# A one-column exponential ahead of ScalarE's DMA issues, and one weight slice issued by SyncE instead of ScalarE

## The chip, the core and the metric

The kernel runs on one core of one Trainium2 chip. The metric is the device time of one execution in microseconds (us), from several executions of the same program; the median is compared. The core has five engines that work in parallel, each with an instruction stream of its own: TensorE (PE, matrix products and transposes), VectorE (DVE), ScalarE (ACT, element functions such as exp and gelu, each from a function table that must be loaded), GpSimd (POOL) and SyncE (SP, which here only issues transfers). Engines meet through semaphores. A transfer (DMA) between the chip's memory and the core's on-chip memory is issued by an instruction of SyncE, ScalarE or GpSimd and carried out by sixteen DMA engines that all queues share.

## The reference: what is computed

The input x has 2048 rows (tokens) of 640 values. Two branches are computed from it and mixed by a gate per token, g = sigmoid(sum(x * gate_w)):

```
q, k, v   = x @ wqkv, in 32 heads of 20;  phi(t) = (t+1 if t>0 else exp(t)) + 1e-6
branch A  = ((phi(q) @ (phi(k)^T v)) / (phi(q) . sum phi(k) + 1e-6)) @ wo
h         = gelu(layernorm(x) @ w1), its four column groups shifted by 1, -1, 2, -2 tokens
x1        = x + h @ w2
branch B  = x1 + gelu(layernorm(x1) @ w3) @ w4
out       = g * A + (1 - g) * B
```

All tensors are bf16; sums run in float32.

## The kernel before, in words

Tokens are worked in 16 tiles of 128 rows, and in four chunks of four tiles where a weight stands still in TensorE. Weights of 640 input rows are cut in five slices of 128 rows. First come the products for q and k (with exp on ScalarE and the rest of phi on VectorE), then the sums over tokens of branch A, then w1 and w2 of branch B, then w3, and last the products with w4 and with the folded matrix of branch A, which add into the same result.

How the order is made: the class `_Sched` records every operation with its reads and writes, derives the semaphore waits from them, and keeps a rough cost for each (a cost model, in `simulate`). The class `_Items` lists work items in streams with dependences and takes, step by step, the item that can start soonest by these costs. The stream "A" (q and k) is a fixed order. An exp whose table is not the one last used is costed 1290 ns more in `activation` (the variable `act_func`). Each engine gets its instructions in the order in which they were recorded; a semaphore wait in a stream holds what stands behind it in that stream.

The beginning, which the change touches, is written out by hand, ahead of the planner:

- `load_x(t)` issues the 160 KB of tile t of x on SyncE; `load_wq(k, queue)` issues 128 KB (the first 512 columns of slice k of the q weights, tile `wq`) on the queue named; `load_wk(k, queue)` 160 KB of the k weights (tile `wkg`). `x_turn(t)` has a DMA transpose x tile t into `xT`, on SyncE, and waits for that tile.
- SyncE's order is x0, x1, wq2, x2, wk0, wk2, x3, wk4, x4, then turn 3 (which waits for x3), x5, turn 4, and chunks of x with their turns. ScalarE's is wq0, wq1, wq3, wq4, wk1, wk3, and the last 128 columns of all wq slices in one transfer (here called wqt); then its own computing begins. GpSimd issues the small row gate_w.
- Beside it TensorE runs dummy products (`warmup`, line 904) and then `t_x` (line 637), which transposes an x tile by a product with the identity; VectorE copies the result into `xT` (line 691). Tiles 0 to 2 go this way, later ones by `x_turn`.
- `q_three` (line 942 through `stream`) is a hand-written order of q's products for tiles 0 to 2, one step per tile and slice:

```
order = [(0, 0), (1, None), (0, 1), (1, 0), (1, 1), (0, 2), (1, 2), (0, 3), (1, 3), (2, None), (0, 4), (1, 4),
         (2, 0), (2, 1), (2, 2), (2, 3), (2, 4)]
```

Here (t, k) is tile t times slice k, which needs wq slice k and the transposed part k of tile t, and (t, None) is the transposes of tile t, which need x tile t. TensorE works this list in order: a step that waits holds all behind it. Then `k_two` does tiles 0 and 1 of k in the same manner, and single tiles follow.
- `phi` does exp on ScalarE out of PSUM (line 682) and two VectorE operations.

Lines 281 and 285 are the helper that issues DMAs (transposes and plain ones); all of them carry these line numbers.

Of the kernel before, what the change touches and what calls it, by code (L numbers as in the profile page):

```python
# [6 lines left out]
F32 = mybir.dt.float32  # L7
ACTF = mybir.ActivationFunctionType
# [408 lines left out]
def _build(nc, A_x, A_wqkv, A_wo, B_w1, B_w2, B_w3, B_w4, gate_w, out, dbg=None, stop=None):  # L417
# [66 lines left out]
    junk = pa.alloc("junk", [128, 1, D], BF16)  # L484
# [78 lines left out]
    def nfree(ap):  # L563
        n = 1
        for d_ in ap.shape[1:]:
            n *= d_
        return n

    def in_psum(ap):
        return ap.tensor.name == ps.name  # L570

    def act(fn, reads, writes, cost=None):
        if cost is None:
            n = nfree(writes[0])
            cost = max(150.0, 100.0 + 0.833 * n + (70.0 if (reads and in_psum(reads[0])) else 0.0))
            cost += 45.0 * max(0, len(reads) - 1)
        return sch.op("act", fn, reads, writes, cost=cost)

    def dve(fn, reads, writes, cost=None):
        if cost is None:  # L580
            n = nfree(writes[0])
            cost = 65.0 + n / 0.96
        return sch.op("dve", fn, reads, writes, cost=cost)
# [85 lines left out]
    def activation(out_ap, in_ap, func, scale=1.0, bias=0.0, accum=None):  # L669
        rd = [in_ap] + [a for a in (scale, bias) if not isinstance(a, (int, float))]  # L670
        wr = [out_ap] + ([accum] if accum is not None else [])
        n = nfree(out_ap)
        cost = max(150.0, 100.0 + 0.833 * n + (70.0 if in_psum(in_ap) else 0.0)) + 45.0 * (len(rd) - 1)
        if accum is not None:
            cost += 91.0
        st_ = ACT_SET.get(func)
        if st_ is not None and st_ != sch.act_func:
            cost += 1290.0
            sch.act_func = st_
        if accum is not None:  # L680
            return act(lambda e: e.activation(out_ap, in_ap, func, bias=bias, scale=scale, accum_out=accum), rd, wr, cost=cost)  # L681
        return act(lambda e: e.activation(out_ap, in_ap, func, bias=bias, scale=scale), rd, wr, cost=cost)  # L682
# [16 lines left out]
    def dma_in(out_ap, in_ap, key, **kw):  # L699
        return sch.dma("sp", out_ap, in_ap, key, **kw)  # L700

    def load_x(t):
        dma_in(x_tok[:, t, :], x2[128 * t:128 * (t + 1), :], "x%d" % t)

    def load_wq(k, queue):
        sch.dma(queue, wq[:, k, 0:512], A_wqkv[128 * k:128 * (k + 1), 0:512], "wq%d" % k)
# [6 lines left out]

    gwr = xn[:, 1, 0:128]
    dve(lambda e: e.memset(gwr, 0.0), [], [gwr])
    load_x(0)
    load_wq(0, "act")
    load_x(1)
    load_wq(1, "act")
    load_wq(2, "sp")  # L720
# [730 lines left out]
def bass_gated_mix__linear_attn_block__mixer_s_mlp__prompt_kernel(  # L1451
    nc, A_x, A_wqkv, A_wo, B_x, B_w1, B_w2, B_w3, B_w4, gate_w, out
):
    assert tuple(A_x.shape) == (1, S, D) and tuple(out.shape) == (1, S, D)
    assert tuple(A_wqkv.shape) == (D, 3 * D) and tuple(A_wo.shape) == (D, D)
    assert tuple(B_w1.shape) == (D, D) and tuple(B_w2.shape) == (D, D)
    assert tuple(B_w3.shape) == (D, F) and tuple(B_w4.shape) == (F, D) and tuple(gate_w.shape) == (D,)
    _build(nc, A_x, A_wqkv, A_wo, B_w1, B_w2, B_w3, B_w4, gate_w, out)
# [28 lines left out]
```

## Time and profile before

| | us |
|---|---|
| median of three runs | 258.79 (258.46 to 259.11) |
| the profiled execution | 259.12 |
| its span, first to last instruction | 257.9 |
| TensorE busy | 254.6 (99% of the span) |
| VectorE / ScalarE / GpSimd busy | 144.1 / 108.5 / 90.6 |
| first product of q's list starts | 4.32 |
| x tile 2's transposes start | 7.28 |
| function table loads on ScalarE | 2 of 1.28, at 4.14 and at 68.30 |

The span of the profile lies 1.2 us under the execution's own time. A profile names engines as PE, PEld (weight loads of TensorE), DVE, ACT, POOL and SP; SPq and ACTq are the queues of SyncE and ScalarE, where a line is the issue of a DMA and not its transfer. In a timeline a line has the start, the length, the engine, the line of the kernel, the operation, out<-in with the shapes, how many were merged, and in brackets how long the engine had been idle before it and what released it. Matmuls are pipelined, so the length of one is longer than the distance to the next.

### The profile page before, as it was taken

To read this page: it belongs to the slowest core of one execution; us is meant where nothing else is said; L and a number is where in the kernel's file an instruction comes from. 1 tells how busy PE (TensorE), PEld (TensorE's weight loads), DVE (VectorE), ACT (ScalarE), POOL (GpSimd) and SP (SyncE) were. 2 spreads that over 40 slices of the span, in tenths; PEclk is the share of its full clock that TensorE was granted. 3 is DMA by queue.
4 is the path that set the end of the run, shared out by engine and by line. 5 is a ranking of instruction groups with operands and counts; after the bars stand their busy time and mean duration, and the time that the engine had idled before them with its cause. 6 is when DMAs were issued, how large, how long until landed. Compare 5 with 4: busy or idle time off the path is not lost.

```text
span 257.9 us, 3612 instructions
## 1 busy us (share of the span) xinstructions
PE 254.6 (99%) x1418; PEld 110.6 (43%) x1242; DVE 144.1 (56%) x290; ACT 108.5 (42%) x222; POOL 90.6 (35%) x146
## 2 busy tenths in 40 slices
PE   8999999999999999999999999999999999999997
PEld 4333333344454333334444444444444444444444
DVE  2697888899953995489999400689300043200033
ACT  1486676751356867665854230003520100253000
POOL 5021399967762153758907100423000011300000
DMA  6767698545843699362915520022300112200002
GB/s 209 223 170 197 145 144 223 172 86 127 108 99 78 97 335 382 85 106 51 124 40 127 127 54 20 0 82 73 51 0 0 23 20 102 102 1 3 0 20 102
DMA packets 57825, 26.48 MB, mean 103 GB/s; under 512 B 49188, under 2 KB 56397, under 8 KB 57808
## 3 DMA queue, kind: packets, MB, share of 16 engines
q1 hardware_dynamic: 54976, 21.87, 35.9%
q0 software_dynamic: 1168, 3.28, 4.9%
q10 hardware_dynamic: 1664, 1.11, 1.4%
q8 instruction: 10, 0.16, 0.3%
q14 instruction: 7, 0.06, 0.1%
HBM read 12.04 MB, written 2.62 MB: 57 GB/s over the span
## 4 chain that ended last, share of the span: by engine, by line
PE 96%; DMA 2%; SPq 0%; DVE 0%; issue 0%
PE ps L606 37%; PE ps L1240 30%; PE ps L625 14%; PE ps L831 7%; PE ps L614 4%; DMA x_tok<-in_A_x_dram 2%; PE ps L942 1%; PE ps L1286 1%; PE ps L1147 1%; SPq L285 0%; PE ps L1029 0%; PE ps L1058 0%; PE ps L637 0%; DVE x_tok L665 0%
## 5 line engine op out<-in xcount | busy, mean ns | idle before, releaser
L606 PE MATMUL ps<-xnT,w 128*128 128x512 bf16 x360 | 81.3, 379 | 0.0
L665 DVE SCALAR_TENSOR_TENSOR x_tok<-ps,stg,abx 128x512 bf16<-128x512 f32 (+2 forms) x17 | 12.2, 719 | 81.5 <-PE ps L1240 81.3
L682 ACT ACTIVATE h2T<-ps 128x512 bf16<-128x512 f32 x52 | 30.6, 598 | 59.3 <-PE ps L606 59.3
L606 PEld LDWEIGHTS ps<-xnT,w 128*128 128x128 bf16 x360 | 34.5, 98 | 41.6 <-issue 2.2
L1240 PE MATMUL ps<-w,h2T 128*128 128x512 bf16 (+2 forms) x221 | 45.4, 366 | 0.0
L648 POOL TENSOR_SCALAR xn<-x_tok,st 128x640 bf16<-128x640 bf16 x32 | 35.3, 1110 | 27.8 <-DMA xnT<-xn 27.2
L648 POOL TENSOR_SCALAR abx<-x_tok,stg 128x640 f32<-128x640 bf16 (+1 forms) x16 | 14.8, 930 | 70.0 <-DVE x_tok L665 70.0
L1240 PEld LDWEIGHTS ps<-w,h2T 128*128 128x128 bf16 x221 | 21.1, 98 | 24.1
L682 ACT ACTIVATE Er<-ps 128x512 bf16<-128x512 f32 (+1 forms) x36 | 23.0, 648 | 14.8 <-PE ps L614 10.6
L681 ACT ACTIVATE junk<-x_tok 128x640 bf16<-128x640 bf16 x32 | 23.6, 738 | 3.9 <-DVE x_tok L663 3.7
L682 ACT ACTIVATE hsT<-ps 128x512 bf16<-128x512 f32 (+1 forms) x32 | 19.0, 593 | 12.6 <-PE ps L606 12.1
L625 PE MATMUL ps<-w,hsT 128*128 128x512 bf16 x80 | 23.0, 379 | 0.0
L625 PE MATMUL ps<-wkg,xT 128*128 128x512 bf16 x70 | 20.6, 379 | 0.0
L663 DVE SCALAR_TENSOR_TENSOR x_tok<-ps,x_tok 128x640 bf16<-128x640 f32 x16 | 13.2, 822 | 10.8 <-PE ps L614 10.2
L1240 PE MATMUL ps<-M_sb,pqnT 128*128 128x512 bf16 (+2 forms) x85 | 18.6, 367 | 0.0
L831 PE MATMUL ps<-pk_tok,x_tok 128*128 128x512 bf16 x80 | 17.8, 379 | 0.0
L614 PE MATMUL ps<-wkg,xT 128*128 128x130 bf16 x80 | 17.6, 220 | 0.0
L1176 DVE TENSOR_TENSOR pq_tok<-pq_tok,dnr 128x300 bf16<-128x300 bf16 (+1 forms) x48 | 17.3, 415 | 0.6
L614 PE MATMUL ps<-w,hsT 128*128 128x128 bf16 x80 | 17.5, 219 | 0.0
L606 PE MATMUL ps<-wq,xT 128*128 128x512 bf16 x65 | 16.2, 379 | 0.0
L648 DVE TENSOR_SCALAR Er<-Er 128x512 bf16<-128x512 bf16 (+1 forms) x36 | 12.2, 340 | 6.8 <-ACT Er L682 5.9
L656 DVE TENSOR_TENSOR qprod<-qprod,pk_tok 128x640 f32<-128x640 f32 x13 | 15.1, 1165 | 0.4
(90 smaller groups left out, 252.4 us busy)
## 6 DMA issues: line engine op xcount, KB each, us to landing
w<-in_B_w_dram SPq DMA_DIRECT2D x1, 2160.0 KB, 8.1
w<-in_B_w_dram SPq DMA_DIRECT2D x1, 2080.0 KB, 13.1
out_dram<-x_tok SPq DMA_DIRECT2D x3, 640.0 KB, 3.1
w<-in_B_w_dram POOLq DMA_DIRECT2D x8, 160.0 KB, 3.4
x_tok<-in_A_x_dram SPq DMA_DIRECT2D x6, 160.0 KB, 4.1
x_tok<-in_A_x_dram SPq DMA_DIRECT2D x1, 960.0 KB, 5.5
wv<-in_A_wqkv_dram POOLq DMA_DIRECT2D x1, 800.0 KB, 5.3
x_tok<-in_A_x_dram SPq DMA_DIRECT2D x1, 640.0 KB, 5.0
```

Source lines behind the costliest of these rows:

```text
L606: ins = e.matmul(out_ap, l, r, start=(i == 0), stop=(i == n - 1))
L614: return e.add_instruction(mybir.InstMatmult(name=nc.get_next_instruction_name(), engine=e.engine, ins=[e.lower_ap(r), ll], outs=[e.lower_ ...
L625: e.matmul(outs[0], l, r, start=st, stop=sp, skip_group_check=True)
L648: return engf(lambda e: e.tensor_scalar(out_ap, in_ap, s1, s2, op0, op1), rd, [out_ap], cost=cost)
L656: return engf(lambda e: e.tensor_tensor(out_ap, a, b_, op), [a, b_], [out_ap], cost=cost)
L663: return dve(lambda e: e.scalar_tensor_tensor(out_ap, in0, scalar, in1, op0, op1, accum_out=accum), rd, [out_ap, accum], cost=cost + 70.0)
L665: return dve(lambda e: e.scalar_tensor_tensor(out_ap, in0, scalar, in1, op0, op1), rd, [out_ap], cost=cost)
L681: return act(lambda e: e.activation(out_ap, in_ap, func, bias=bias, scale=scale, accum_out=accum), rd, wr, cost=cost)
L682: return act(lambda e: e.activation(out_ap, in_ap, func, bias=bias, scale=scale), rd, wr, cost=cost)
L831: ins = e.matmul(o, l, r, start=(t0 + q_ == 0), stop=(t0 + q_ == NT - 1))
L1176: dve(lambda e, o=o, i0=i0, i1=i1: e.tensor_tensor(o, i0, i1, ALU.mult), [i0, dnr[:, 1, sd, :]], [o], cost=cost)
L1240: ins = e.matmul(o, l, r, start=first and i == 0, stop=last and i == len(prs) - 1, skip_group_check=True)
```

## The change

A one-column exponential of a constant zero is put ahead of ScalarE's DMA issues, into the scratch tile `junk`, whose contents nobody reads. So the first instruction of ScalarE that needs a table stands ahead of its first DMA issue. And wq's slice 0 is issued by SyncE behind x tile 0, where ScalarE issued it first of all.

```
     gwr = xn[:, 1, 0:128]
     dve(lambda e: e.memset(gwr, 0.0), [], [gwr])
+    activation(junk[:, 0, 0:1], nc.const_aps.tensor(0.0, [128, 1], F32), ACTF.Exp)
     load_x(0)
-    load_wq(0, "act")
+    load_wq(0, "sp")
     load_x(1)
     load_wq(1, "act")
     load_wq(2, "sp")
```

With it SyncE's order begins x0, wq0, x1, wq2, x2, wk0, and ScalarE's is table load, exponential, wq1, wq3, wq4, wk1, wk3, wqt.

More of the change, by code (lines that the diff above doesn't have):

```diff
@@ L715, in _build @@
     dve(lambda e: e.memset(gwr, 0.0), [], [gwr])
+    activation(junk[:, 0, 0:1], nc.const_aps.tensor(0.0, [128, 1], F32), ACTF.Exp)
     load_x(0)
-    load_wq(0, "act")
+    load_wq(0, "sp")
     load_x(1)
```

## The prediction

> **What bounds the kernel now.** I read the page's busy times first, then who TensorE waited for over the whole span, then the chain of work that ended last, and then the first 14 us instruction by instruction.
>
> ```profile
> PE 254.6 (99%) x1418; PEld 110.6 (43%) x1242; DVE 144.1 (56%) x290; ACT 108.5 (42%) x222; POOL 90.6 (35%) x146
> ...
> PE ps L904 <- PEq L1472: 0.8, 1, 0.8
> PE ps L637 <- DMA x_tok<-in_A_x_dram: 0.6, 1, 0.6
> ```
>
> The first line is the page's; the other two are the complete list of TensorE's waits. TensorE is the bound, and it has two waits: 0.8 us for the program's start, and one for a transfer of x. By the distances between its matmuls it loses nothing more than a tenth of a microsecond at a time from 7.3 us to its end. So whatever delays TensorE in the first 9 us comes out at the end in full, and no change of the opening can gain more than the second wait and a few tenths around it.
>
> ```profile
> 2.18 5.05 DMA x_tok<-in_A_x_dram
> 7.28 0.45 PE ps L637 x5
> 7.74 1.82 PE ps L942 x8
> ```
>
> The chain shows the wait: x tile 2, issued at 2.18, lands 5.05 us later, and its transposes (L637) start at 7.28. The last product before them started at 6.35 (trace) and products stand 0.216 apart, so the gap is 7.28 - 6.56 = 0.72 us.
>
> ```profile
> 0.79 0.87 SPq L285 DMA_DIRECT2D x_tok<-in_A_x_dram  x2
> 0.79 1.86 ACTq L285 DMA_DIRECT2D wq<-in_A_wqkv_dram  x4
> 1.71 0.43 SPq L285 DMA_DIRECT2D wq<-in_A_wqkv_dram  x1
> 2.18 0.43 SPq L285 DMA_DIRECT2D x_tok<-in_A_x_dram  x1
> 2.66 0.91 SPq L285 DMA_DIRECT2D wkg<-in_A_wqkv_dram  x2
> 4.14 1.28 ACT L682 ACT_TABLE_LOAD   x1 [4.14 <-issue]
> 8.01 1.09 ACT L682 ACTIVATE Er<-ps 128x512 bf16<-128x512 f32 x2 [2.59 <-PE ps L942]
> ```
>
> The timeline shows two queues issuing side by side, one DMA per 0.47 us each, and the table load as soon as ScalarE's seven issues are over. It ends at 5.42; the first exp waits for TensorE until 8.01.
>
> ```profile
> x_tok<-in_A_x_dram SPq DMA_DIRECT2D x1, 160.0 KB, 3.1
> wq<-in_A_wqkv_dram SPq DMA_DIRECT2D x1, 128.0 KB, 3.6
> ...
> x_tok<-in_A_x_dram SPq DMA_DIRECT2D x1, 160.0 KB, 5.1
> wkg<-in_A_wqkv_dram SPq DMA_DIRECT2D x1, 160.0 KB, 5.5
> wq<-in_A_wqkv_dram ACTq DMA_DIRECT2D x1, 128.0 KB, 5.3
> ```
>
> These are DMA issues with the time to landing (issues in flight around 1.6 us, then around 2.5 us): x1 and wq2, then x2, wk0 and wq4. Issue plus latency gives landings, and the n-th DMA of SyncE lands together with the n-th of ScalarE: x0 3.7 with wq0 3.8; x1 4.4 with wq1 4.6; wq2 5.3 with wq3 5.6; x2 7.3 with wq4 7.5; wk0 8.16 with wk1 8.3. I call these slots 1 to 5. From 2 us on the DMA engines are 93 to 112% busy by windows of 1 us, so a landing is set by the bytes that go before it on both queues, not by its issue.
>
> **The change part by part.**
>
> *The table load and the exponential.* The load (1.28 us) leaves 4.14 and comes to about 0.79. This gains nothing: ScalarE waits 2.59 us for TensorE ahead of its first exp even now. The exponential itself is bounded by 0.17 us (the two-column copy of lr, 174 ns). What hides both is ScalarE's idleness until 8.01; uncovered they would cost 1.45 us. The question is what they do to the six DMA issues that now stand behind them.
>
> *ScalarE's six issues (wq1, wq3, wq4, wk1, wk3, wqt).* No row before has an issue behind a table load. One end: the issues don't wait, and wq1 is issued at about 0.9 instead of 1.23. The other: they wait until the engine is ready again. The second table load bounds that from above, as the next ACTIVATE began 71.14 - 68.30 = 2.84 us after it started:
>
> ```profile
> 68.30 1.28 ACT L682 ACT_TABLE_LOAD   x1
> 71.14 0.60 ACT L682 ACTIVATE hsT<-ps 128x512 bf16<-128x512 f32 x1 [1.56 <-PE ps L606]
> ```
>
> In the middle lies a hold of the load and the exponential, 1.28 + 0.17 = 1.45 us, with wq1 issued at about 2.2. I take no hold. The nearest records are the trace's semaphore instructions of ScalarE: one is done at 29.19, while the read of an accumulator that stands ahead of it in the stream starts only at 29.39, and one at 11.57, with an ACTIVATE running from 11.56 to 12.26. So ScalarE's instruction stream runs on ahead of its computing, and a DMA issue is, like them, an instruction that needs no function unit.
>
> The Trainium skill agrees with this row and speaks against the change: Trace Analysis, "DVE / Act Engine Instruction", has the sequencer push such an instruction into a queue and fetch the next, and its section on DMA instructions starts an issue on the sequencer once its semaphores are there. By this rule the hold is 0. Another page (ScalarE: Activation LUTs, "What ACT_TABLE_LOAD costs") speaks of 2.66 us with a drain; were the issues behind that, wq1 would go out at 3.5 us. No run here shows either for a DMA issue.
>
> *wq0 moves to SyncE.* One more issue on SyncE moves x1, wq2, x2, wk0, wk2, x3, wk4 and x4 by 0.47 us each, which alone is little. But each moves back by a slot too. SyncE's order becomes x0, wq0, x1, wq2, x2: x2 goes from slot 4 to slot 5, where wk0 is now. The five slots hold the same bytes as before (288 + 256 + 288 + 288 + 320 = 1440 KB against 288 + 288 + 256 + 288 + 320), so slot 5 ends at the same 8.16. Along `q_three`, which TensorE works in order:
> - (0,0) needs wq0, slot 2: 4.4 to 4.5 instead of 3.8, used at 4.32. About 0.1 late.
> - (1,None) needs x1, slot 3: 5.3 instead of 4.4, used at 4.39. 0.9 late, and wq1, which came earlier, waits with all behind it.
> - (0,2) needs wq2, slot 4: 7.3 instead of 5.3, used at about 5.7. Then four steps at 0.216, so (1,3) ends at 7.3 + 0.86 = 8.16.
> - (2,None) needs x2, slot 5: 8.16. Both are there at once, and the transposes start at 8.16 instead of 7.28: **0.88 us** late.
>
> Behind it nothing is added: wq4 has landed a slot earlier, wk0 lands in slot 6 (8.9, where wk2 is) for a use at 9.2 + 0.88, and wk4 at 10.6 (where x4 is) for 11.1 + 0.88. On SyncE turn 3 waits for x3, which goes from 9.5 to slot 8, 10.1 (where wk4 is). Turn 3 thus moves from 9.55 by 0.6, and so do x5, turn 4 and the chunks behind it; turn 3 lands at 12.6 instead of 12.0, and TensorE wants it at 13.2 + 0.88. SyncE's extra issue is hidden by its idleness from 5.2 to 9.5. GpSimd's issue of gate_w is passed by nothing.
>
> *Sum:* 0 (table, exponential) + 0.88. On the profiled execution 259.12 + 0.88 = 260.0; that one was 0.33 above the median, so by the median 258.79 + 0.88 = **259.67**. Ends of this case: 0.6, if the slowest DMA engine is less behind (half of x2's sixteen parts had landed by 6.1, the last at 7.23), and 1.1, if wq2 lands with the later partner of its slot (7.5).
>
> **The rivals.**
>
> *The issues are held for 1.45 us (not slower).* With wq1 at 2.2 SyncE has the DMA engines alone until data of ScalarE's start to flow, about 1.2 us after an issue (wq0, issued at 0.79, has its first packets near 2.0). SyncE's delay of one DMA (128 KB at half of some 330 GB/s, 0.8 us) is made good by a hold of 0.8 us, and that is the point from which this rival decides. Then x2 lands near 6.8; wq1 lands 3.3 us after its issue (its latency now) at 5.5 instead of 4.6; seven steps to (1,3) end at 5.5 + 1.51 = 7.0, x2's transposes start 0.25 early, and (0,4) waits for wq4, issued at 3.2 and due at 7.4 to 7.8 (now 7.60). Between -0.25 and +0.2: 258.5 to 259.0. For it speaks that ScalarE's first load started just after the issues ended, in stream order; against it the semaphore records.
>
> *They are held for up to 2.84 us.* wq1 at 3.7, landing at 6.7 to 7.0; seven steps to 8.2 to 8.5, transposes and (0,4) at 8.5 to 8.8 instead of 7.60: +0.9 to +1.2, 259.7 to 260.0. Nothing in the rows needs so long a hold.
>
> *TensorE's pace stays slow.* Five transposes take 0.71 us at 3.71 and 0.44 us at 4.64: the pace doubles near 4.5 us, after 3.7 us of unbroken work, though the granted clock reads 1.00 throughout. In my forecast TensorE idles from about 4.6 to 5.3, right there, and again ahead of wq2. If the faster pace doesn't come or is lost, four steps after wq2 take 0.43 each, +0.86, and the rest of q's list, nine products, up to 9 x 0.21 = 1.9 more: 260.5 to 262.4.
>
> The Trainium skill (TensorE: Matmul & The Clock Gate, Part 1) has the gate judge activity over free-running windows of about 3.4 us, and close after an idle one. No window here would be wholly idle, so by that rule the pace once gained is kept.
>
> *The planner writes another order.* Its costs now put the 1290 ns of the table ahead and ScalarE's issues later, so a later item can change its place. As TensorE has no waits to give up behind 9 us, this could only lose; 0 to 1 us, 258.8 to 259.8.
>
> **How the numbers follow.** No hold 0.55; short hold 0.28; long hold 0.07; slow pace 0.06; another order 0.04. A measurement can tell about 0.3% here, 0.78 us. No hold (0.6 to 1.1, mid 0.88) is over it two times in three: 0.36 slower, 0.19 same. Short hold: 0.24 same, 0.02 each side. Long hold 0.045 slower, 0.025 same. Slow pace: slower. Another order 0.025 slower, 0.01 same, 0.005 faster. Sums: slower 0.51, same 0.46, faster 0.03. The likeliest case's own range is 259.4 to 259.9; the range must take in the short hold down to 258.4, and above it the long hold and some of the slow pace, to 260.5.
>
> **What would show it.** In the changed profile: a first line of ScalarE's queue near 0.9 (no hold), 2.2 or 3.7; the table load near 0.79 and the first exp still released by TensorE; x2 landing near 8.1 and L637's third group of transposes starting there, with TensorE's waits in sum about 0.9 us longer, on x1, wq2 and x2; transposes of tile 1 at 0.056 or 0.107 apart. I am wrong if ScalarE's first issue comes after the table load: then x2's transposes start at or before 7.3 and the time stays.

## The result and the profile after

| | before | after |
|---|---|---|
| median of 12 runs each, us | 259.07 (258.32 to 259.48) | 259.89 (259.49 to 261.56) |
| ratio, 95% interval | | 1.0049 (1.0031 to 1.0067) |
| the profiled execution / its span | 259.12 / 257.9 | 261.08 / 259.8 |

The changed kernel is slower: +0.82 us between the medians, and by the ratio 259.07 x 0.0049 = 1.27 us (0.8 to 1.7). The two numbers differ because the runs after lie in two groups: seven from 259.49 to 259.91, one at 260.45, and four from 260.94 to 261.56. The runs before have one group. The profiled execution after, 261.08, belongs to the upper one.

The beginning of its timeline, ScalarE and its queue, and SyncE's queue:

```profile
0.79 1.28 ACT L682 ACT_TABLE_LOAD   x1 [0.79 <-PEq L1473]
0.79 0.40 SPq L285 DMA_DIRECT2D x_tok<-in_A_x_dram  x1
0.86 1.35 ACTq L285 DMA_DIRECT2D wq<-in_A_wqkv_dram  x3
1.26 0.41 SPq L285 DMA_DIRECT2D wq<-in_A_wqkv_dram  x1
1.71 0.43 SPq L285 DMA_DIRECT2D x_tok<-in_A_x_dram  x1
2.08 0.21 ACT L682 ACTIVATE junk<-const-float32-0.0 128x1 bf16<-128x1 f32 x1
2.18 0.43 SPq L285 DMA_DIRECT2D wq<-in_A_wqkv_dram  x1
2.23 0.94 ACTq L285 DMA_DIRECT2D wkg<-in_A_wqkv_dram  x2
2.66 0.43 SPq L285 DMA_DIRECT2D x_tok<-in_A_x_dram  x1
...
10.10 1.08 ACT L682 ACTIVATE Er<-ps 128x512 bf16<-128x512 f32 x2 [7.82 <-PE ps L943]
```

ScalarE's queue starts at 0.86, 0.07 us behind the start of the table load and 1.2 us ahead of its end: the load doesn't hold the DMA issues behind it. The exponential follows at 2.08, as soon as the load ends. ScalarE then idles 7.82 us until TensorE has something for it. (The Trainium skill, ScalarE: Activation LUTs, "What ACT_TABLE_LOAD costs", counts a drain of 1.38 us to such a load; here 0.01 us lie between the load and the next ACTIVATE.)

TensorE in the same timeline (start, length, idle before):

```profile
3.66 0.74 PE L637 MATMUL ps<-ident,x_tok 128*128 128x128 bf16 x5
4.20 0.31 PE L905 MATMUL ps<-const-bfloat16-1.0 128*128 128x128 bf16 x1
4.35 0.59 PE L943 MATMUL ps<-wq,xT 128*128 128x512 bf16 x1
5.70 0.72 PE L637 MATMUL ps<-ident,x_tok 128*128 128x128 bf16 x5 [0.76 <-DMA x_tok<-in_A_x_dram]
6.21 3.19 PE L943 MATMUL ps<-wq,xT 128*128 128x512 bf16 x7
9.19 0.63 PE L637 MATMUL ps<-ident,x_tok 128*128 128x128 bf16 x5
9.69 1.74 PE L943 MATMUL ps<-wq,xT 128*128 128x512 bf16 x7
```

The same in the profile before:

```profile
4.64 0.44 PE L637 MATMUL ps<-ident,x_tok 128*128 128x128 bf16 x5
4.95 1.78 PE L942 MATMUL ps<-wq,xT 128*128 128x512 bf16 x7
7.28 0.45 PE L637 MATMUL ps<-ident,x_tok 128*128 128x128 bf16 x5 [0.55 <-DMA x_tok<-in_A_x_dram]
7.60 1.74 PE L942 MATMUL ps<-wq,xT 128*128 128x512 bf16 x7
```

Two things are to be seen. x1's transposes start at 5.70 (4.64 before), with TensorE idle ahead of them. And the seven products after them take 3.19 us, where seven take 1.74 in the last line: their starts stand 0.427 apart instead of 0.216. TensorE is at half its pace until about 9.5. So x2, landed since 8.35, is taken up only at 9.19, and (0,4) starts at 9.69 instead of 7.60: 2.09 us late. The span is 1.9 us longer.

The chain confirms that the beginning now hangs on x1 and not on x2:

```profile
1.71 3.95 DMA x_tok<-in_A_x_dram
5.65 0.05 issue
5.70 0.72 PE ps L637 x5
6.42 2.99 PE ps L943 x7
9.40 0.42 PE ps L637 x5
```

Apart from the table load, the exponential and wq0's issue, the order of the recorded instructions on every engine is the same as before.

### The profile page after: what moved, and what is told of

It reads as the page before. It is cut to its first block, busy times and chain, and to the rows that moved or that the text cites. A ratio compares the mean times of both kernels' runs of the same rounds, so it can differ in the third digit from the quotient of the medians.

```text
span 259.8 us, 3586 instructions
## 1 busy us (share of the span) xinstructions
PE 254.7 (98%) x1391; PEld 111.4 (43%) x1242; DVE 143.5 (55%) x290; ACT 108.7 (42%) x223; POOL 90.8 (35%) x146
## 4 chain that ended last, share of the span: by engine, by line
PE 95%; DMA 2%; ACT 1%; issue 1%; SPq 0%; DVE 0%
PE ps L606 36%; PE ps L1241 30%; PE ps L625 13%; PE ps L832 7%; PE ps L614 4%; PE ps L943 3%; DMA x_tok<-in_A_x_dram 2%; PE ps L1287 1%; ACT hsT L682 1%; PE ps L1148 1%; PE ps L637 0%; PE ps L1030 0%; PE ps L1059 0%; ACT junk L681 0%; SPq L285 0%
## 5 line engine op out<-in xcount | busy, mean ns | idle before, releaser
L606 PE MATMUL ps<-xnT,w 128*128 128x512 bf16 x348 | 79.9, 379 | 0.6 <-issue 0.2
```

Of the source, the lines that this page charges most:

```text
L606: ins = e.matmul(out_ap, l, r, start=(i == 0), stop=(i == n - 1))
```

## The experiments

Theory at their start: (1) the early table load costs nothing; (2) the move of wq0 puts x1, wq2 and x2 a slot back, where the n-th DMA of a queue lands in the n-th slot; (3) in some runs the idle stretch while x1 is late leaves TensorE at its slow pace, and these are the upper group. Rivals: the table load costs; a later issue costs only its 0.47 us; the upper group has later transfers and not a slower TensorE. The kernel before ran beside the experiments on each chip, and ratios are to those runs.

### One part alone: the move, and the exponential

```
 e1:  -    load_wq(0, "act")
      +    load_wq(0, "sp")
 e2:  +    activation(junk[:, 0, 0:1], nc.const_aps.tensor(0.0, [128, 1], F32), ACTF.Exp)
           load_x(0)
           load_wq(0, "act")
```

> Only wq0 moves to SyncE; no early exponential, so ScalarE's first issue is wq1 at 0.79 us. Slot theory (the move puts x1, wq2 and x2 one slot back, the early table load costs nothing): the time of the changed kernel, 259.9 us in the median, with x2 landing at 8.1 to 8.4, and again a second group of runs near 261. Rival (the table load ahead of the issues is what costs): back to 259.1.

> Only the early exponential; wq0 stays on ScalarE. Slot theory: ScalarE's first issue goes from 0.79 to 0.86 and every slot stays, so 259.1 us (0 to +0.1). Rival (the table load ahead of the issues is what costs): 259.9.

| | median | all runs | ratio to before |
|---|---|---|---|
| e1, move only | 261.05 (7 runs) | 259.66 to 259.94 three times, 261.05 to 261.78 four times | 1.0073 (1.0046 to 1.0100) |
| e2, exponential only | 258.80 (12 runs) | 258.16 to 259.18 | 0.9995 (0.9986 to 1.0005) |

The move alone makes the loss, in both groups. Its median falls in the upper group because four of seven runs do; I had expected the median of the lower one. The exponential alone costs nothing that can be told: the interval ends at +0.13 us. In its profile, too, ScalarE issues under the load:

```profile
0.79 1.28 ACT L682 ACT_TABLE_LOAD   x1 [0.79 <-PEq L1473]
0.86 1.35 ACTq L285 DMA_DIRECT2D wq<-in_A_wqkv_dram  x3
2.08 0.20 ACT L682 ACTIVATE junk<-const-float32-0.0 128x1 bf16<-128x1 f32 x1
...
6.39 0.44 PE L637 MATMUL ps<-ident,x_tok 128*128 128x128 bf16 x5
```

The last line is x2's transposes, without a wait: x2 lands at 6.25 here and at 7.23 in the profile of before, from the same place in its queue. A landing thus moves by up to 1 us from one execution to another, and a single profile's landings are no exact base for a sum.

### One transfer a slot back: x2, and x1

```
 e4:       load_wq(3, "act")
      -    load_x(2)
           load_wq(4, "act")
           load_wk(0, "sp")
      +    load_x(2)
 e5:  -    load_x(1)
      +    load_wq(2, "sp")
           load_wq(1, "act")
      -    load_wq(2, "sp")
      +    load_x(1)
```

> The kernel before with x2 and wk0 exchanged on SyncE: x2 alone goes from slot 4 to slot 5, x1 and wq2 stay. Slot theory: x2 lands at 8.1 to 8.2 us and its transposes start there, +0.88, 259.95 us. Rival (a later issue moves a landing by the 0.47 us of the issue): +0.47, 259.5. The idle stretch comes when TensorE has long been at its fast pace; by the pace theory none of the runs falls into a group near 261.

> The kernel before with x1 and wq2 exchanged on SyncE: x1 alone goes from slot 2 to slot 3, wq2 comes earlier, x2 stays in slot 4. Pace theory: TensorE idles from 4.6 to 5.3 us. Where it gets its fast pace all the same, (1,3) ends near 7.3 and x2 is there, 0 to +0.2, 259.1 to 259.3; where it doesn't, seven products at 0.427 put x2's transposes to about 9.1, +1.9, near 261; some runs of each. Rival (an idle stretch here has no effect on the pace): all runs at 259.1 to 259.3.

e4: 259.98 in the median, 259.77 to 260.58 in ten runs, ratio 1.0033 (1.0019 to 1.0046), so +0.86 us (0.5 to 1.2) on 259.19. The slot's 0.88 is met; the issue's 0.47 lies only just under the interval. No run is near 261. TensorE in its profile:

```profile
4.78 0.94 PE L942 MATMUL ps<-wq,xT 128*128 128x512 bf16 x3
7.00 1.13 PE L942 MATMUL ps<-wq,xT 128*128 128x512 bf16 x4 [1.29 <-DMA wq<-in_A_wqkv_dram]
8.59 0.45 PE L637 MATMUL ps<-ident,x_tok 128*128 128x128 bf16 x5 [0.45 <-DMA x_tok<-in_A_x_dram]
8.90 1.31 PE L942 MATMUL ps<-wq,xT 128*128 128x512 bf16 x5
```

x2 lands at 8.54 here (8.16 expected). A wait that I had not expected is that for wq2: it keeps its place in the queue, yet lands at 6.96, where it landed at 5.34 in the profile of before.

e5: 260.94 in the median, 259.26 to 261.95 in ten runs, ratio 1.0068 (1.0046 to 1.0090). Only x1 is later, x2 keeps slot 4, and five of ten runs lie over 260.9: the upper group is there without x2 being moved at all, so the rival that expected 259.1 to 259.3 falls. The lower runs are later than the 259.1 to 259.3 that I gave them, though: x1 landed at 6.15, not 5.3.

### Dummy work while x1 is late

If TensorE's pace is what makes the upper group, work that fills the idle stretch must remove it, though every transfer is issued as before. Between q's first product and x1's transposes, 256 dummy columns are put in six or eight times:

```
-        order = [(0, 0), (1, None), (0, 1), ...
+        order = [(0, 0), *[(None, None)] * 6, (1, None), (0, 1), ...
```

e3 is the changed kernel with six, e9 with eight. e8 is e5 with eight, and e5b repeats e5 on the same chip beside it.

> The changed kernel with 1536 more dummy columns on TensorE between q's first product and x1's transposes, so that TensorE has work while x1 is late. Pace theory (the runs near 261 are those in which the idle stretch at 4.6 to 5.7 us kept TensorE at its slow pace): the distance of 512-column products is 0.216 us from about 5 us on in every run, 259.5 to 260.0 in all runs, none over 260.3. Rival (those runs have later transfers): the spread stays, 259.5 to 261.5.

> The kernel with x1 and wq2 exchanged once more, as the partner on the same chip of the next one. Both theories: as measured, 260.9 us in the median with runs from 259.3 to 262.

> The same with 2048 dummy columns between q's first product and x1's transposes; the transfers are issued as in its partner. Pace theory: TensorE is busy while x1 is late, the pace doubles by about 5 us in every run, and the upper runs go: 259.3 to 260.3, no run over 260.6, median 259.8. Rival (the upper runs come from late transfers or anything else that dummy work doesn't touch): 260.9 again, up to 262.

> The changed kernel with 2048 dummy columns at the same place. Pace theory: no run over 260.6, and what remains over the kernel before is the slots: x2 a slot later, +0.9 (+0.6 to +1.1). Rival: runs near 261 to 261.5 as in the changed kernel.

| | median | highest | runs over 260.9 | ratio to before |
|---|---|---|---|---|
| changed kernel | 259.89 | 261.56 | 4 of 12 | 1.0049 (1.0031 to 1.0067) |
| e3, with six | 260.20 | 260.79 | 0 of 6 | 1.0051 (1.0034 to 1.0068) |
| e9, with eight | 260.02 | 260.53 | 0 of 12 | 1.0034 (1.0021 to 1.0048) |
| e5b, x1 late | 260.06 | 261.75 | 4 of 12 | 1.0048 (1.0026 to 1.0070) |
| e8, the same with eight | 260.02 | 260.76 | 0 of 11 | 1.0035 (1.0020 to 1.0050) |

Without the dummy work 17 of 41 runs (changed kernel, e1, e5, e5b) are over 260.9, with it 0 of 29. The bound of 260.9 was set after the runs were seen; at 260.6 it would be 18 of 41 and 3 of 29. Some of the bounds I had set beforehand were tighter: e3 has two runs over 260.3 and e8 two over 260.6. The repeat, e5b, has fewer upper runs than e5 (4 of 12, 5 of 10), so its median is not the 260.9 expected. e9's +0.34% is 0.88 us (0.5 to 1.2) on 259.04: what remains over the kernel before without the upper group. It is the slots' part, with whatever the dummy work itself costs, which wasn't measured apart. By an estimate from the distances of 0.107 us, sixteen pieces at the slow pace hold TensorE for 1.7 us, from 4.7 to 6.4, while x1 lands at 5.65 in the changed kernel's profile.

How the pace goes is seen in e5b's profile, an execution of 261.57. First TensorE's timeline:

```profile
3.66 0.48 PE L637 MATMUL ps<-ident,x_tok 128*128 128x128 bf16 x5
4.24 0.39 PE L942 MATMUL ps<-wq,xT 128*128 128x512 bf16 x1
6.41 0.45 PE L637 MATMUL ps<-ident,x_tok 128*128 128x128 bf16 x5 [1.78 <-DMA x_tok<-in_A_x_dram]
6.70 2.86 PE L942 MATMUL ps<-wq,xT 128*128 128x512 bf16 x7
9.36 0.74 PE L637 MATMUL ps<-ident,x_tok 128*128 128x128 bf16 x5
9.96 1.95 PE L942 MATMUL ps<-wq,xT 128*128 128x512 bf16 x7
```

Then two stretches of it (us of the window; busy time of PE, PEld, DVE, ACT and POOL; granted clock; share of the DMA engines; GB/s):

```profile
3.74:7.15 3.41, 1.59 (x16) 0.81 (x14) 1.12 (x5) 1.28 (x1) 0.90 (x6) 1.00 0.86 244
7.15:10.56 3.41, 3.41 (x14) 1.54 (x14) 0.63 (x5) 0.00 (x0) 0.00 (x0) 0.50 0.98 327
```

The five transposes at 3.66 take 0.48 us, those at 6.41 take 0.45, and those at 9.36 take 0.74. So the pace had doubled by 3.8, held through 1.8 us of idleness, and was halved after it, from 7.15 to 10.56, with a granted clock of 0.50. In that stretch TensorE is busy all the time and gets half as much done. In the profiles of the changed kernel and of e1 the pace stayed at half from the start until 9.5 and 9.8, with 1.00 written as the clock throughout; there the distance of the products is what shows it.

A wait of 1.29 us, in e4, did not halve it. The stretch that corresponds to e5b's first one:

```profile
3.78:7.19 3.41, 2.08 (x17) 1.03 (x17) 1.36 (x5) 1.28 (x1) 0.87 (x5) 1.00 0.89 253
```

TensorE is busy for 2.08 us of it, where e5b had 1.59, and the products behind it, from 8.90 on, stand 0.22 to 0.27 apart and not 0.43.

With the dummy work, in e9:

```profile
4.30 0.64 PE L943 MATMUL ps<-wq,xT 128*128 128x512 bf16 x1
4.73 1.26 PE L905 MATMUL ps<-const-bfloat16-1.0 128*128 128x128 bf16 x16
6.35 0.45 PE L637 MATMUL ps<-ident,x_tok 128*128 128x128 bf16 x5 [0.36 <-DMA x_tok<-in_A_x_dram]
6.64 1.80 PE L943 MATMUL ps<-wq,xT 128*128 128x512 bf16 x7
8.28 0.44 PE L637 MATMUL ps<-ident,x_tok 128*128 128x128 bf16 x5
```

x1 lands at 6.30, even later than in the changed kernel's profile, and still x2's transposes start at 8.28 and not at 9.19, since the seven products run at 0.216. Later transfers don't make the upper group.

### The issues held behind the exponential

The rival that was to end on the other side needs a hold that the chip doesn't make. It can be made by a semaphore: ScalarE's first issue waits for the exponential.

```
-    activation(junk[:, 0, 0:1], nc.const_aps.tensor(0.0, [128, 1], F32), ACTF.Exp)
+    first = activation(junk[:, 0, 0:1], nc.const_aps.tensor(0.0, [128, 1], F32), ACTF.Exp)
...
-    load_wq(1, "act")
+    load_wq(1, "act", [first])
```

> The changed kernel, but ScalarE's first issue waits for the exponential to be done, so it starts near 2.3 us. By the rival of the prediction (a hold of 1.45 us makes good the move of wq0): -0.25 to +0.2 on before, 258.8 to 259.3 us, with x2's transposes at 7.0 to 7.3. If a hold makes nothing good, the time of the changed kernel or more, 259.9 to 261.

259.97 in the median, 259.11 to 261.26 in nine runs, ratio 1.0043 (1.0023 to 1.0063). The rival's 258.8 to 259.3 is missed. Its profile:

```profile
2.32 1.35 ACTq L285 DMA_DIRECT2D wq<-in_A_wqkv_dram  x3
5.15 0.45 PE L637 MATMUL ps<-ident,x_tok 128*128 128x128 bf16 x5 [0.42 <-DMA x_tok<-in_A_x_dram]
6.01 1.67 PE L943 MATMUL ps<-wq,xT 128*128 128x512 bf16 x7 [0.40 <-DVE xT L691]
7.52 0.44 PE L637 MATMUL ps<-ident,x_tok 128*128 128x128 bf16 x5
8.25 1.04 PE L943 MATMUL ps<-wq,xT 128*128 128x512 bf16 x4 [0.28 <-DMA wq<-in_A_wqkv_dram]
```

(The edit is against the changed kernel; load_wq hands the list on to the DMA.) SyncE's transfers are in large part made good: x1 lands at 5.11 and x2 at 6.26. But on ScalarE's queue wq1 lands at 5.87 instead of 5.5, and wq4, now third behind a held queue, at 8.20 instead of 7.4 to 7.8; it holds (0,4) until 8.25, 0.65 us after 7.60. In this execution, 259.67, the hold moved the lateness from one queue to the other. Two of the nine runs, 261.18 and 261.26, belong to the upper group; x1's transposes are late here too, 5.15 instead of 4.64.

### The other way: x2 a slot earlier

```
-    load_wq(2, "sp")
-    load_wq(3, "act")
     load_x(2)
+    load_wq(2, "act")
+    load_wq(3, "sp")
     load_wq(4, "act")
...
+        order = [(0, 0), (1, None), (0, 1), (1, 0), (1, 1), (2, None), (0, 2), (1, 2), (2, 0), (2, 1), (2, 2),
+                 (0, 3), (0, 4), (1, 3), (1, 4), (2, 3), (2, 4)]
```

> The other way: SyncE issues x0, x1, x2, wq3 and ScalarE wq0, wq1, wq2, wq4, and q's list does tile 2's transposes after (1,1) and the nine products with slices 0 to 2 before those with slices 3 and 4. So TensorE has one product and one set of transposes more, 0.5 us, for the time until slot 4 lands (7.3 to 7.5). Slot theory: -0.5 us, 258.6, with no idle stretch over 0.3 us. Rival (the slots don't follow the order of issue so simply, and x2 or wq2 comes late in slot 3): 259.1 or more.

258.88 in the median, 258.52 to 259.36 in twelve runs, ratio 0.9992 (0.9981 to 1.0003). That is -0.2 us with an interval that reaches to +0.1, so no gain is shown, and the 0.5 expected is the interval's far end. In its profile slot 3, with x2 and wq2, lands at 6.56 and 6.75, as its rival had it, and TensorE waits ahead of it instead of ahead of slot 4: 0.54 us by the line, 0.71 by the distance of its products.

```profile
6.61 0.45 PE L637 MATMUL ps<-ident,x_tok 128*128 128x128 bf16 x5 [0.54 <-DMA x_tok<-in_A_x_dram]
```

## Why the prediction was right, and where it was wrong

**The outcome.** 259.67 was forecast and 259.89 measured, in the range of 258.4 to 260.5; slower was the likelier side. That the median lies so near is in part luck: the eight lower runs alone have a median of 259.82, the four upper ones lie 1.1 to 1.7 us above it, and with e1's share of upper runs, four of seven, the median would have been outside the range.

**The hold.** Right: no hold was taken, 0.9 for the first issue, and 0.86 came. ScalarE's semaphore records were the right sign.

**The table load and the exponential at nothing.** Right: 0.9995 in e2. The exponential took 0.21 us, a little more than its bound of 0.17.

**wq0's move, +0.88 by the slot.** Right in size where TensorE's pace is kept: 0.88 (0.5 to 1.2) in e9, and 0.86 in e4 where x2 alone is moved. x2 in slot 5 was put at 8.16 and came at 8.35 (after), 8.01 (e9) and 8.54 (e4). But in the profiles with x1 late the waits of the sum are not the ones that came: x1, wq2 and x2 were forecast, and in the changed kernel, e1, e3 and e9 TensorE waits for x1 alone. The forecast had wq2 at 7.3; it lands at 6.75 in the changed kernel and at 7.15 in e9, ahead of its use. So in e9 the size agrees although x1's path, and not the one that was added up, ended last; that is luck.

**x1 in slot 3 at 5.3.** Mis-sized: 5.65 in the changed kernel, 6.09 in e1, 6.30 in e9, 6.43 in e3. The 5.3 was one landing of one execution. Slot 3 ends between 5.0 (e2) and 7.0 us (e4) over these profiles, set by the last of a transfer's sixteen parts. So x1's own path is as long as x2's was to be: in e9 6.30, then 1.98 us to the end of (1,3), 8.28. In e3 and e9 it ends last, where the prediction had x2 and wq2.

**The slow pace, chance 0.06.** The mechanism and its price were right (260.5 to 262.4 against 260.94 to 261.56), and its chance was mis-sized: 4 of 12 runs, and 17 of 41 with the other kernels that make x1 late. The step that failed weighed the idle stretch at 0.9 us behind 4.4, and leaned on a rule. In the profiles the doubling falls anywhere from 3.7 (e3) to 5.1 us (e9) where TensorE is kept busy, so the idle stretch can come ahead of it and put it off (to 9.5 in the changed kernel), or take it away again afterwards (e5b). The Trainium skill (TensorE: Matmul & The Clock Gate, Part 1) has the gate close after an idle window of about 3.4 us. e5b's clock fell to 0.50 after 3.41 us in which TensorE was busy for 1.59, so here the measurement decides: a window that is half idle was enough.

**The short hold, 258.5 to 259.0.** Wrong in e6's profile by its term for wq4: 8.20 against 7.4 to 7.8. It also left out the upper group, 2 of 9 runs there.

**Another order by the planner.** It didn't happen.

**What stays open.** Why the last part of SyncE's slot 3 lands 0.15 us behind the median part in one execution (e2) and 1.7 in another (e3) wasn't tried. The dummy work shows that filling the idle stretch takes the upper runs away; that a window's busy share decides is inferred from the profiles (1.59 of 3.41 us halved the pace, 2.08 didn't), and its threshold wasn't measured.

## What to carry to other kernels

Moving a DMA issue to another queue costs every transfer behind it there a place, even where it frees one in the queue that it leaves: with both queues backed up, count places in each queue up to the transfer that the compute engine waits for, and not issue times. A function table load ahead of DMA issues on ScalarE costs them next to nothing, but it is also no gain where ScalarE idles before its first exp anyway. A wait of 0.8 to 1.8 us in TensorE's first 6.5 us can cost twice, once as the wait and once as half pace after it, in some runs only; look at the distance between products in the profile, and compare all runs, not the median alone.

## What the runs showed of the hardware that was not expected

- The granted clock fell to 0.50 for 3.4 us (7.15 to 10.56 in e5b) after 1.8 us of idleness, though the pace had already doubled.
- ScalarE's first DMA issue started 0.07 us after its table load did, and the exponential 0.01 us after the load's end.
- The same transfer at the same place in its queue (wq2 before, in e2 and in e4) landed at 5.34, 5.02 and 6.96 us.
